# A planner's order searched anew, a shorter wait for the first weight combinations, and unit 1's layernorm statistics on another engine

## The chip, the cores and the metric

The kernel runs on one core of a Trainium2 chip. A core has a matrix engine (TensorE, PE in the profile; its weight loads are shown as PEld), a vector engine (VectorE, DVE), a scalar engine (ScalarE, ACT), a general engine (GpSimd, POOL) and a sync engine (SyncE, SP), which here does little but issue transfers. Each engine works through its own list of instructions in order and waits on semaphores; transfers run on 16 DMA engines. The metric is the device time of one execution in microseconds, as the median of several runs.

## The reference

Two layers, each of them a block of dilated local attention and a feed-forward block, on 2048 tokens of 1024 features. Each query looks at 8 keys, at distances 0, 2, ..., 14 behind it.

```python
def _layernorm(x, axis=-1, eps=1e-5):
    m = jnp.mean(x, axis=axis, keepdims=True)
    v = jnp.var(x, axis=axis, keepdims=True)
    return (x - m) / jnp.sqrt(v + eps)

def _A_ref(x, wqkv, wo):                      # H = 32, Dh = 32, W = 8, dil = 2
    qkv = (x @ wqkv).reshape(B, S, 3, H, Dh)  # then split into q, k, v by head
    idx = pos[:, None] - jnp.arange(W) * dil
    kg, vg = k[idx], v[idx]                   # idx < 0 is masked
    logits = jnp.einsum("bhsd,bhswd->bhsw", q, kg) * Dh ** -0.5
    o = jnp.einsum("bhsw,bhswd->bhsd", softmax(logits), vg)
    return o @ wo

def _B_ref(x, w1, b1, w2, b2):                # F = 3584
    r = relu(x @ w1 + b1)
    return (r * r) @ w2 + b2

x = A_x
x = x + _A_ref(_layernorm(x), A_wqkv, A_wo)
x = x + _B_ref(_layernorm(x), B_w1, B_b1, B_w2, B_b2)
x = x + _A_ref(_layernorm(x), A_wqkv, A_wo)
x = x + _B_ref(_layernorm(x), B_w1, B_b1, B_w2, B_b2)
```

## The kernel before

**Units.** The tokens are split into even and odd ones, so that the dilation becomes a window of 8 neighbours, and then into blocks of 512. A layer has four blocks, so there are eight units, 0 to 7; a unit has four tiles of 128 tokens. A unit passes through: `SA` (load x, layernorm, transpose into `xnA`), `SQ` or `SQ7` (the products for q, k and v), `S2` (attention), `SW` or `SW7` (the output projection with wo, the residual, the second layernorm, transpose into `xnB`), `SF1` (first feed-forward product, relu, square) and `SF2` (second one, and the output). The attention of unit u+1 is woven into the feed-forward block of unit u: attention is VectorE's work, the products are PE's.

**Seven products.** Most matrix products are done as 2 x 2 blocks with seven block products instead of eight. For that, sums and differences of weight blocks are needed. They are made once, from the weights as they are first loaded, by VectorE into tiles `tv` (lines L531 for wqkv, L680 for w1, L457 for w2, L1108 for wo), stored to scratch tensors in DRAM (`sk`, `sqv`, `sw`, `tw`, `two`), and loaded again by later units. The sums and differences of the other operand are the tiles `T` (L699) and `TA` (L703). For the k weights this is done in unit 0 by `keep_wqkv`: eight combinations of 128 x 1024, each followed by a store of 256 KB.

**The opening.** Unit 0's tiles are taken in the order 0, 1, 3, 2. Tiles 0, 1 and 3 get their statistics on VectorE (BATCH_NORM_STATS2 at L791, aggregate at L793) and are normalised there (L788); tile 2 goes over ScalarE. All four are transposed on PE (L807) and copied to `xnA` (L812, named `ptc` in the plan).

**Layernorm, two ways.** `ln` has a flag `vec`. With it, VectorE makes the statistics (two of L732 and one of L741 for each tile), ScalarE the inverse root (L736, L737), VectorE the normalisation (L740). Without it, ScalarE makes the statistics in two passes over the tile with a sum beside each (L746, L750, each with a read of the accumulator; L747 between them) and the inverse root (L753, L754); VectorE normalises (L759). In `SW` and `SW7` the flag is `u in STAT`. The transposes of later units are DMA transposes issued by SP (L772).

**Logits.** `S2` multiplies q with the shifted k in 16-bit products `P` (L950, 128 x 2048), eight of them for each half block, adds them up in a tree of depth `DEP0[hb]` for unit 0 (L958), and sums what is left over the features on PE with a matrix of ones (L965, four matmuls for each remaining tile). With depth 2, two tiles are left of eight; with depth 3, one.

**The order.** Nothing is issued as the functions run. Each operation is recorded in a `Plan` with an engine, a duration, what it reads and writes and a priority. `emit` first disturbs the priorities with a list of seeds (`shift`), lets `schedule` place the operations on the engines by a simple model with a limited number of buffers, and then, for each further list in `ORDER`, takes the start times of that placement as priorities, disturbs them again (`reshift`) and places anew. The last placement is the order of the instructions in every engine's list, SP's transfers included, and it also decides which buffer each tile gets. So the seeds in `ORDER` decide all orders, and nothing else in them does anything. A search outside the kernel found them.

Lines that the prediction speaks of: L663 are the matmuls of all seven-product steps, L888 those of the plain q, k, v products, L1084 those of the output projection, L485 and L1388 those of the second feed-forward product, L1057 the copies out of PSUM (`yxa`, `yxo`, `yxm`) that feed the residual additions, L1496 the difference of the two halves of the bias b2 (`b2d`), L422 every plain transfer. `xt` are the x tiles loaded for the first layernorm of a unit.

Of the kernel before, what the change touches and what calls it, by code (L numbers as in the profile page):

```python
# [26 lines left out]
ONPE = (0,)  # L27
FOLD = (0, 1, 2)
DEN = (0,)
STAT = (1, 2, 3, 4, 5, 6, 7)  # L30
NORM = (3,4,5,6,7)
EQ = True
QW = 1
# [12 lines left out]
KEEP = {"k": 0, "q": 1, "v": 1}  # L46
WO7 = (2, 3, 4, 5, 6)
KWO = 1
DEP0 = (2, 2)
NEARLY = 4  # L50
PLAIN1 = 1
HALF = 8
# [6 lines left out]
AGF = True  # L59
FNO = True  # L60
CPA = (1,)
TAIL = True
CPT = ("xn3",)
PR1 = 20.0
# [3 lines left out]
GZ = 6  # L68

ORDER = [  # L70
# [6 lines left out]

MM = 0.2157
MMH = 0.1091
# [10 lines left out]
def act(n):  # L90
    return 0.05 + n * 0.00084
# [242 lines left out]
class _Kernel:  # L334
# [465 lines left out]
    def transpose(self, xn, xnT, tl, prio, parts=1, act=False):  # L800
# [3 lines left out]
        for i in range(parts):  # L804
# [3 lines left out]

            on_act = act or parts > 1 and i in CPA

# [16 lines left out]
    def SA(self, u):  # L827
        p = self.p
        layer, b = divmod(u, self.NB)
        st = self.state.setdefault(u, {})  # L830
        xnT = Buf("8K", "xnA1" if u == 1 else "xnA", [128, 4, self.KD, 128], F16)
        st["xnA"] = xnT
        after = [self.state[u - 2].get("gatef") or self.state[max(u - 2, 1)].get("gatev")] if u >= 2 else ()
        first, rst = (), []
        for tl in ORD if u == 0 else range(4):
            t = b * 4 + tl
            x, xv = self.load_x(layer, t, after, tag="x0" if u == 0 else "xt", prio=PR1 if u == 1 else -1e6 if u == 0 else None,
                                eng="ACT" if u == 0 and tl in XACT else "SP")
            if u == 0 and tl in LNA:
                self.ln(x, xv, [0], xnT, tl, LNP, False, on_pe=True, tag="xn3", after=rst, vnorm=tl in LNV)  # L840
            elif u == 0:
                bn, ag, r, rest = self.ln_first(x, xv, xnT, tl, first)
                rst.append(r)
                if tl == 0:
                    first, rest0 = [ag] if AGF else [bn], rest
                elif tl == 1:
                    rest0([ag])
                    c, xn, no = rest()
                    first = [no if FNO else c]
                    self.keep_clock(NPB, xn)  # L850
                else:
                    rest()
            else:
                self.ln(x, xv, [0], xnT, tl, PR1 if u == 1 else 20.0, False, vnorm=u in NORM)

    def SQ(self, u, jobs, order=None, halves=()):
        nc, p = self.nc, self.p
        layer, b = divmod(u, self.NB)
        KD, NCH, D = self.KD, self.NCH, self.D
        st = self.state[u]  # L860
        xnT = st["xnA"]
        offs = {"q": 0, "k": HALO, "v": HALO}
        ws = {}
        for nm in jobs:
            self.qkv_buf(u, nm)
            ws[nm] = [Buf("8K", "w", [128, 2, 2, 4, 256], BF) for _ in range(2)]
        pieces = u == 0 and len(jobs) > 1
        for ms in range(4) if pieces else (0, 2):
            for nm in jobs:
                w = ws[nm][ms // 2]  # L870
                if pieces:
                    self.dma(lambda w=w, ms=ms: w[:, ms % 2].rearrange("p a k n -> p (a k n)"), lambda nm=nm, ms=ms: self.wqkv_block(nm, ms), (),
                             [(w, ms % 2)], 0.53, name="w")
                else:
                    self.dma(lambda w=w: w[:].rearrange("p s a k n -> p s (a k n)"),
                             lambda nm=nm, ms=ms: self.wqkv_block(nm, ms, 2).rearrange("(s p) m -> p s m", p=128), (), [(w, 0), (w, 1)], 1.06, name="w")
        if order is None:
            order = [(nm, c0) for nm in jobs for c0 in range(NCH)]

        def chunk(nm, c0, hs, parts=1):  # L880
            pq = Buf("ps", "pq", [128, BLK], F32)
            w, dst, off = ws[nm][c0 // 4], st[nm], offs[nm]
            t0, t1 = hs[0], hs[-1] + 1
            n = KD // parts

            def fm(i):
                for kd in range(i * n, (i + 1) * n):
                    nc.tensor.matmul(pq[:, t0 * HB:t1 * HB], w[:, c0 // 2 % 2, kd // 4, kd % 4, c0 % 2 * 128:c0 % 2 * 128 + 128],  # L888
                                     xnT[:, 2 * t0:2 * t1, kd, :], start=(kd == 0), stop=(kd == KD - 1))
            for i in range(parts):  # L890
                xc = [(xnT, t if i == parts - 1 else (t, i)) for t in range(2 * t0, 2 * t1)]
                st["gate" + nm] = self.pe(4 * len(hs) / parts, lambda i=i: fm(i), xc + [(w, c0 // 2 % 2)], [(pq, h) for h in hs], name="pq")
            p.add("ACT", act(HB * len(hs)), lambda: nc.scalar.copy(dst[:, c0, off + t0 * HB:off + t1 * HB], pq[:, t0 * HB:t1 * HB]),
                  [(pq, h) for h in hs], [(dst, (c0, h)) for h in hs], 2.0, name="cast")

        for nm, c0 in halves:
            chunk(nm, c0, (0,), 2 if (nm, c0) == halves[0] else 1)
        for nm, c0 in order:
            chunk(nm, c0, (0, 1))
            yield  # L900
        for nm, c0 in halves:
            chunk(nm, c0, (1,))
        for nm in jobs:
            if u == KEEP[nm]:
                self.keep_wqkv(nm, ws[nm], [op for op in self.p.ops if op.name == "ptc"] if u == 0 else ())
            self.halo_out(u, nm)

    def qkv_buf(self, u, nm):
# [152 lines left out]
    def SW(self, u):  # L1061
# [12 lines left out]
        for tl in range(4):  # L1074
# [18 lines left out]
            st["xm"].append(xm)  # L1093
            self.ln(xm, lambda xm=xm: xm[:], [0, 1], xnT, tl, 1.0, u in STAT, on_pe=u in ONPE)
        if u == KWO:
# [21 lines left out]
    def SW7(self, u):  # L1117
# [25 lines left out]
        def cells(k2, m2):  # L1143
            return [(o, (k2 * h + c, m2)) for c in range(h)]
# [6 lines left out]
        def mul(left, lc, w, right, bank, start):  # L1151
            for q in range(2):
                def fm(q=q):
                    for j in range(h):
                        nc.tensor.matmul(bank[q][:], left(j, q), right(j), start=start and j == 0, stop=j == h - 1, skip_group_check=True)  # L1155
                self.pe(h, fm, lc + [(w, 0)], [(bank[q], 0)], name="py")

        def block(k2, m2):
            return lambda j, q: o[:, k2 * h + j, m2 * HB + q * 128:m2 * HB + (q + 1) * 128]

        def T(i):
            return ts[i // 2], lambda j: ts[i // 2][:, i % 2, j, :]
# [31 lines left out]
        for q in range(2):  # L1194
            self.ln(xm[q], lambda q=q: xm[q][:], [0, 1], xnT, q, 1.0, u in STAT, on_pe=u in ONPE)
        mul(block(0, 1), cells(0, 1), *T(2), X, False)
# [5 lines left out]
        for q in range(2):  # L1202
            self.ln(xm[q + 2], lambda q=q: xm[q + 2][:], [0, 1], xnT, q + 2, 1.0, u in STAT, on_pe=u in ONPE)

# [154 lines left out]
    def SF2(self, u):  # L1359
# [21 lines left out]
        def mul(name, left, lcells, banks, start, split=False):  # L1381
            for half in range(2):
                w = self.w2_rhs(name, half)
                for q in range(2):
                    def fm(lo=0, hi=BLK, w=w, q=q, half=half):
                        for j in range(g):
                            jj = half * g + j
                            nc.tensor.matmul(banks[q][:, lo:hi], left(jj, q), w[:, j, lo:hi], start=(start and jj == 0), stop=(jj == h - 1),  # L1388
                                             skip_group_check=True)
                    if split and half and q and TAIL:  # L1390
                        xr = xm[3]
# [58 lines left out]
    def out_tile(self, layer, t, db, py, xm, end=False):  # L1450
# [5 lines left out]
        o = lambda: xm[:].bitcast(BF)  # L1456
        if end and TAIL:
            for i in range(2):
# [54 lines left out]
    def build(self):  # L1513
# [9 lines left out]
        self.biases()  # L1523
        self.S2(0, DEP0)
        for u in range(NU):
# [88 lines left out]
```

## Time and profile before

| | |
|---|---|
| median of 3 runs | 1137.02 us (1135.94 to 1138.26) |
| the profiled execution | 1142.31 us |
| its span, first to last instruction | 1140.6 us |
| PE, DVE, ACT busy | 1121.8, 995.5, 814.0 us |
| moved by DMA | 362.35 MB, mean 318 GB/s |
| granted TensorE clock, mean | 0.999 |

The profile is of one execution. Its page gives busy time by engine, then the span in 40 equal slices of 28.5 us with a digit for the busy tenths of each, then queues, the chain of work that ended last, and the costliest groups of instructions. A group's line shows the source line, the engine, what is written and read, the shapes, the count, then busy time and mean duration, then the time for which the engine idled just before such instructions and what ended that. A line of waits reads: engine, tile and line that waited, what it waited for, total us, times, longest. A matmul's own mean (379 ns for 128 x 512) is longer than its share of busy time, since matmuls overlap.

### The profile page before, as it was taken

To read this page: it belongs to the slowest core of one execution; us is meant where nothing else is said; L and a number is where in the kernel's file an instruction comes from. 1 tells how busy PE (TensorE), PEld (TensorE's weight loads), DVE (VectorE), ACT (ScalarE), POOL (GpSimd) and SP (SyncE) were. 2 spreads that over 40 slices of the span, in tenths; PEclk is the share of its full clock that TensorE was granted. 3 is DMA by queue.
4 is the path that set the end of the run, shared out by engine and by line. 5 is a ranking of instruction groups with operands and counts; after the bars stand their busy time and mean duration, and the time that the engine had idled before them with its cause. 6 is when DMAs were issued, how large, how long until landed. Compare 5 with 4: busy or idle time off the path is not lost.

```text
span 1140.6 us, 20659 instructions
## 1 busy us (share of the span) xinstructions
PE 1121.8 (98%) x7857; PEld 771.2 (68%) x7904; DVE 995.5 (87%) x1528; ACT 814.0 (71%) x1628; POOL 1.8 (0%) x8
## 2 busy tenths in 40 slices
PE   8999999998999999999999999999999999999998
PEld 6645864676846787468864688557884678845864
DVE  7999999998997899979999699995999989996341
ACT  7747896566984689757994669847698478943961
POOL 0000000000000000000000000000000000000000
PEclk9999999999999999999999999999999999999999
DMA  9965699999999996999879997899979999589981
GB/s 356 285 217 220 225 317 291 346 343 342 364 339 386 345 377 228 333 396 328 357 281 322 412 335 303 309 310 393 359 271 325 372 354 413 209 304 313 367 299 62
DMA packets 137022, 362.35 MB, mean 318 GB/s; under 512 B 67418, under 2 KB 68570, under 8 KB 116570
## 3 DMA queue, kind: packets, MB, share of 16 engines
q1 hardware_dynamic: 136778, 360.95, 91.3%
q8 instruction: 62, 1.02, 0.4%
q14 instruction: 38, 0.31, 0.1%
q10 hardware_dynamic: 144, 0.07, 0.0%
HBM read 314.84 MB, written 31.46 MB: 304 GB/s over the span
## 4 chain that ended last, share of the span: by engine, by line
PE 64%; ACT 12%; DMA 7%; DVE 2%; issue 1%; SPq 0%; ACTq 0%; DVEq 0%
PE X L663 20%; PE X L1388 12%; PE Z L663 10%; PE Z L1388 6%; PE Y L663 5%; PE X L1155 3%; ACT r L1323 3%; PE Y L1388 3%; ACT rr L1329 2%; PE py L1084 2%; PE Z L1155 1%; DMA w<-in_A_wo_dram 1%; DMA w<-sw 1%; DMA xt<-xs 1%; ACT u L1292 1%
## 5 line engine op out<-in xcount | busy, mean ns | idle before, releaser
L663 PEld LDWEIGHTS <-w 128*128 128x128 f16 (+1 forms) x4904 | 480.4, 98 | 75.9 <-DMA w<-sw 3.0
L1388 PEld LDWEIGHTS <-r 128*128 128x128 f16 x1183 | 115.6, 98 | 136.4 <-issue 3.7
L1388 PE MATMUL X<-w,r 128*128 128x512 f16 (+2 forms) x784 | 177.9, 377 | 1.4 <-ACT yxa L1057 1.0
L950 DVE TENSOR_TENSOR P<-q,k 128x2048 f16<-128x2048 f16 x128 | 154.5, 1225 | 2.2 <-ACT q L626 2.0
L663 PE MATMUL X<-T,w 128*128 128x256 f16 x1224 | 154.0, 273 | 0.1
L1029 DVE TENSOR_TENSOR pr<-pb,v 128x4096 f16<-128x4096 f16 x64 | 146.3, 2297 | 0.4 <-PE Z L663 0.2
L958 DVE TENSOR_TENSOR P<-P,P 128x2048 f16<-128x2048 f16 x110 | 134.2, 1220 | 0.1
L1323 ACT ACTIVATE r<-rr 128x1024 f16<-128x1024 f16 x110 | 123.9, 1139 | 0.3
L1036 DVE TENSOR_TENSOR pr<-pr 128x2048 f16<-128x2048 f16 (+1 forms) x128 | 118.0, 954 | 0.0
L663 PE MATMUL X<-TA,w 128*128 128x256 f16 x864 | 107.6, 273 | 0.0
L596 ACT COPY Y<-X 128x512 f32<-128x512 f32 x115 | 70.2, 610 | 26.0 <-PE X L663 21.5
L888 PE MATMUL pq<-xnA,w 128*128 128x256 f16 (+1 forms) x512 | 86.1, 326 | 2.3 <-DMA w<-in_A_wqkv_dram 0.9
L1302 ACT CAST y<-Z 128x512 f16<-128x512 f32 x110 | 69.5, 646 | 10.5 <-PE Z L663 10.1
L888 PEld LDWEIGHTS <-w 128*128 128x128 bf16 x512 | 49.8, 98 | 34.7 <-issue 1.8
L1306 DVE TENSOR_TENSOR rr<-u,y 128x512 f16<-128x512 f16 x110 | 46.1, 423 | 27.7 <-ACT y L1302 12.8
L663 PE MATMUL X<-xnB,w 128*128 128x256 f16 x440 | 56.9, 277 | 0.0
L1329 ACT ACTIVATE rr<-Y,b1T 128x256 f16<-128x256 f32 x110 | 54.4, 537 | 3.1 <-PE Y L663 2.3
L663 PE MATMUL Y<-xnB,w 128*128 128x256 f16 x440 | 56.4, 273 | 0.0
L663 PE MATMUL Z<-T,w 128*128 128x256 f16 x392 | 51.0, 274 | 4.6 <-DMA w<-sw 2.7
L614 ACT CAST u<-X 128x512 f16<-128x512 f32 x72 | 41.7, 586 | 19.3 <-PE X L663 18.5
L1329 ACT ACTIVATE rr<-X,b1T 128x256 f16<-128x256 f32 x110 | 54.6, 560 | 0.3 <-PE X L663 0.3
L618 ACT CAST yq<-Z 128x512 f16<-128x512 f32 x72 | 41.9, 585 | 16.3 <-PE Z L663 16.3
(168 smaller groups left out, 1653.4 us busy)
## 6 DMA issues: line engine op xcount, KB each, us to landing
w<-sw SPq DMA_DIRECT2D x49, 1024.0 KB, 10.2
w<-tw SPq DMA_DIRECT2D x56, 896.0 KB, 6.6
w<-in_B_w_dram SPq DMA_DIRECT2D x42, 896.0 KB, 6.2
w<-in_B_w_dram SPq DMA_DIRECT2D x35, 1024.0 KB, 10.1
w<-in_A_wqkv_dram SPq DMA_DIRECT2D x32, 1024.0 KB, 10.3
w<-sqv SPq DMA_DIRECT2D x24, 1024.0 KB, 10.9
w<-in_B_w_dram SPq DMA_DIRECT2D x28, 512.0 KB, 5.7
w<-sk SPq DMA_DIRECT2D x12, 1024.0 KB, 7.7
```

The lines of the kernel that those rows point to most:

```text
L596: self.p.add("ACT", act(512), lambda: self.nc.scalar.copy(Y[:], X[:]), [(X, 0)], [(Y, 0)], UP, name="u")
L663: nc.tensor.matmul(bank[:, a, :], lw[:, k, a * 128:(a + 1) * 128], rhs(k), start=(start and k == 0 and a == 0), stop=(k == 3), skip_group_ ...
L888: nc.tensor.matmul(pq[:, t0 * HB:t1 * HB], w[:, c0 // 2 % 2, kd // 4, kd % 4, c0 % 2 * 128:c0 % 2 * 128 + 128], xnT[:, 2 * t0:2 * t1, kd, ...
L950: nc.vector.tensor_tensor(cur[:], q[:, c, None, hb * HB:(hb + 1) * HB].to_broadcast([128, W, HB]), _win_ap(k[:, c, :], HALO + hb * HB, HB) ...
L958: nc.vector.tensor_tensor(other[:], other[:], cur[:], ALU.add)
L1029: p.add("DVE", dve(4096), lambda pr=pr, ch=ch: nc.vector.tensor_tensor(pr[:], pb[:].unsqueeze(1).to_broadcast([128, 2, W, HB]), _win_ap2(v ...
L1036: nc.vector.tensor_tensor(dst, pr[:, :, 0:n, :], pr[:, :, n:2 * n, :], ALU.add)
L1302: p.add("ACT", act(512), lambda: nc.scalar.copy(y[:], bank[:]), [(bank, 0)], [(y, 0)], 1.5, name="y")
L1306: p.add("DVE", dve(512), lambda: nc.vector.tensor_tensor(r[:, :, m, :], us[i][:], y[:], ALU.add), [(us[i], 0), (us[i], 1), (y, 0)], [(r, ( ...
L1323: p.add("ACT", 0.955, lambda: nc.scalar.activation(out=r2[:, f:f + 2, :].rearrange("p a t -> p (a t)"), in_=r[:].rearrange("p a m t -> p ( ...
L1329: p.add("ACT", 0.36, lambda a=a: nc.scalar.activation(out=r[:, a, 0, :], in_=bank[:, a, :], func=ACTF.Relu, bias=self.b1T[:, f + a:f + a + ...
L1388: nc.tensor.matmul(banks[q][:, lo:hi], left(jj, q), w[:, j, lo:hi], start=(start and jj == 0), stop=(jj == h - 1), skip_group_check=True)
```

## The change

In the words that come with it: "Order searched anew with every transfer also modelled as landing late; first k combinations wait only for the second tile; unit 1's statistics on VectorE". In the code it is this:

```diff
-STAT = (1, 2, 3, 4, 5, 6, 7)
+STAT = (2, 3, 4, 5, 6, 7)
...
-DEP0 = (2, 2)
+DEP0 = (2, 3)
...
+AFTK = True
...
 ORDER = [
-    [254407839, 254101347, ..., 254651009, ],
-    [254887702, 254542295, ..., 254633564]]
+    [291170133, 291483325, ..., 291274799, ], [291072305, 291809209, ..., 291708481, ],
+    [291835106, 291584461, ..., 291674658, ], [291087832, 291905654, 291120734, 291208902]]
...
                     c, xn, no = rest()
                     first = [no if FNO else c]
+                    self.opened = [no]
                     self.keep_clock(NPB, xn)
...
             if u == KEEP[nm]:
-                self.keep_wqkv(nm, ws[nm], [op for op in self.p.ops if op.name == "ptc"] if u == 0 else ())
+                self.keep_wqkv(nm, ws[nm], () if u else self.opened if AFTK else [op for op in self.p.ops if op.name == "ptc"])
```

- `ORDER` has other seeds: four lists (59, 23, 25 and 4 seeds) in place of two (52 and 23). The order of the instructions on every engine, and the use of buffers, is another one from the opening on. What the search modelled does not stand in the kernel; `schedule` and its constants are the same.
- The k combinations of unit 0 depend on the normalisation of tile 1 (`no`), no longer on the copies of all four transposed tiles.
- Unit 1 is no longer in `STAT`, so in its output projection `vec` is false: the statistics of its second layernorm are made on ScalarE. Before, they were made on VectorE.
- The second half block of unit 0's logits is added up to one tile in place of two: one addition more on VectorE, four matmuls fewer on PE.

All else, the products, transfers and their sizes, is the same.

15 rows, old and new, of the table ORDER are left out of this document.

## The prediction

> **What bounds the kernel now.** I read the page's first part, then busy time by stretches, then the waits of TensorE, then the chain of waits.
>
> ```profile
> span 1140.6 us, 20659 instructions
> PE 1121.8 (98%) x7857; PEld 771.2 (68%) x7904; DVE 995.5 (87%) x1528; ACT 814.0 (71%) x1628; POOL 1.8 (0%) x8
> ```
>
> TensorE (PE) idles for 1140.6 - 1121.8 = 18.8 us in all. That is all an order of instructions can win, beside the few matmuls taken out. Where it idles, and at what clock:
>
> ```profile
> 0.00:15.00 15.00, 11.31 (x78) 6.75 (x79) 8.03 (x23) 8.43 (x21) 1.75 (x8) 1.00 0.87 313
> 15.00:28.50 13.50, 13.50 (x129) 12.05 (x127) 12.17 (x14) 11.85 (x29) 0.00 (x0) 1.00 1.03 404
> 28.50:205.00 176.50, 175.23 (x1072) 104.03 (x1078) 172.98 (x224) 126.94 (x266) 0.00 (x0) 1.00 0.85 263
> 205.00:215.00 10.00, 10.00 (x68) 6.38 (x66) 10.00 (x20) 7.05 (x13) 0.00 (x0) 1.00 0.83 269
> 215.00:250.00 35.00, 33.47 (x244) 23.84 (x244) 35.00 (x53) 21.91 (x45) 0.00 (x0) 1.00 1.07 355
> 250.00:277.00 27.00, 25.09 (x227) 21.87 (x225) 24.07 (x40) 18.90 (x38) 0.00 (x0) 1.00 1.07 327
> 277.00:280.00 3.00, 0.26 (x4) 0.01 (x1) 3.00 (x6) 1.73 (x4) 0.00 (x0) 1.00 1.02 403
> 280.00:285.00 5.00, 5.00 (x31) 3.84 (x32) 3.02 (x4) 2.38 (x5) 0.00 (x0) 0.66 1.01 415
> 285.15:313.67 28.52, 28.47 (x252) 24.57 (x251) 26.89 (x38) 28.49 (x62) 0.00 (x0) 1.00 0.92 364
> 427.73:456.24 28.51, 28.46 (x230) 22.44 (x230) 26.02 (x39) 28.48 (x61) 0.00 (x0) 1.00 0.65 228
> 1112.09:1140.60 28.51, 24.35 (x119) 11.53 (x118) 4.16 (x10) 5.45 (x10) 0.00 (x0) 1.00 0.17 61
> ...
> PE Z L663 <- DMA w<-sw: 2.7, 1, 2.7
> PE Z L663 <- DVE T L699: 1.9, 1, 1.9
> PE py L1084 <- DMA w<-in_A_wo_dram: 1.4, 1, 1.4
> PE X L1388 <- ACT yxa L1057: 1.0, 1, 1.0
> PE pq L888 <- ACT q L893: 0.9, 1, 0.9
> PE Z L1388 <- ACT yxa L1057: 0.3, 1, 0.3
> ```
>
> In the stretches the numbers are length, then busy PE, weight loads, VectorE (DVE), ScalarE (ACT), POOL, then granted clock, DMA share, GB/s. Start (15.00 - 11.31 = 3.7) and tail (28.51 - 24.35 = 4.2) are waits that every order has. What is left is the six waits, 2.7 + 1.9 + 1.4 + 1.0 + 0.9 + 0.3 = 8.2 us, and the stretch behind the longest, where the clock was 0.66: 5.00 x 0.34 = 1.7 us. Three of the waits and the low clock lie between 215 and 285, in unit 1's output projection and first feed-forward product. There the DMA share is at least 1.01 in every row from 215 to 285, so the transfers are the limit, and they land one after another:
>
> ```profile
> 216.29 8.19 DMA w<-in_A_wo_dram
> 251.74 10.78 DMA xnB<-xn
> 264.88 15.06 DMA w<-sw
> 279.99 1.41 PE Z L663 x8
> 735.92 6.87 DMA xt<-xs
> ...
> ACT xn L746 <- DMA xt<-xs: 16.2, 4, 6.0
> ```
>
> The chain of waits (start, length, what) says it in order: the second wo load is issued at 216.29, and the sw load issued at 264.88 took 15.06 us to land, behind the transfers issued before it; PE went on at 279.99. Until about 215 VectorE, not DMA, is full (10.00 of 10.00), and it is VectorE that frees the buffer for the second wo load.
>
> **The point that decides.** In the order of the changed program that same sw load is again first used with 6,088 matmuls still to come, just as many as before. If its landing still holds PE, whatever is won or lost ahead of it is wiped out, and the end moves with the landing. So I cost each part first by what it does to that landing.
>
> **First k combinations (L531).** Before, they waited until all four tiles of unit 0 were transposed; now until the second is normalised. The opening:
>
> ```profile
> 9.56 0.20 DVE L793 BATCH_NORM_AGGREGATE sm<-st 128x2 f32<-128x12 f32 x1
> 10.36 0.55 DVE L788 TENSOR_SCALAR xn<-x,sm 128x1024 f16<-128x1024 bf16 x1 [0.60 <-ACT sm L785]
> 12.54 1.05 PE L888 MATMUL pq<-xnA,w 128*128 128x256 f16 x8 [0.94 <-DMA w<-in_A_wqkv_dram]
> 13.42 0.61 PE L807 MATMUL pt<-ident,xn 128*128 128x128 f16 x8
> 14.07 0.69 DVE L812 COPY xnA<-pt 128x1024 f16<-128x1024 f16 x1 [3.16 <-PE pt L807]
> 19.35 1.29 DVE L531 TENSOR_TENSOR tv<-w 128x1024 f16<-128x1024 bf16 x2
> 25.41 0.69 DVE L1496 TENSOR_TENSOR b2d<-b2b 128x512 f32<-128x512 bf16 x1 [1.29 <-DMA b2b<-in_B_b_dram]
> ```
>
> In the changed order three of them stand on VectorE between the third tile's aggregate (done 9.76) and its normalisation, the fourth behind it. They need the third 512 KB piece of weights; the fourth piece released PE at 12.54, and 0.52 MB at 404 GB/s is 1.3 us, so the third landed near 11.2 (estimate). VectorE waits there from 9.76, works 1.29 + 0.69 until 13.2, normalises until 13.7 and does the fourth by 14.4. Queued behind this wait is the normalisation; PE waits for it. But PE's order has one more group of eight matmuls (1.05) ahead of these transposes: it gets there at about 14.3, not 13.42. So PE is not held, by 0.6 us; without that cover, 13.7 - 13.42 = 0.3. The tile's copy moves from 14.07 to about 15.0: 0.9 later with four combinations done (about 2.6 us), so VectorE is 1.7 us ahead; and b2d, now nine instructions further on, should lose its 1.29 us wait. Together 3.0. The four stores now stand on SP ahead of and among the next weight loads, holding the first of these for some 2 us; its first matmul is behind 200 others, so this costs nothing.
>
> **DEP0 and the statistics.**
>
> ```profile
> L965 PE MATMUL lg<-P,grp 128*128 128x512 f16 x72 | 19.8, 379 | 0.0
> L958 DVE TENSOR_TENSOR P<-P,P 128x2048 f16<-128x2048 f16 x110 | 134.2, 1220 | 0.1
> L732 DVE BATCH_NORM_STATS2 bs<-xm 128x6 f32<-128x512 f16 x56 | 37.8, 689 | 0.5
> L741 DVE BATCH_NORM_AGGREGATE sm<-bs 128x2 f32<-128x12 f32 x28 | 5.5, 204 | 0.2
> L746 ACT ACTIVATE xn<-xm 128x1024 f16<-128x1024 f16 x4 | 4.2, 1051 | 0.0
> L750 ACT ACTIVATE xn<-xm,sm 128x1024 f16<-128x1024 f16 x4 | 4.6, 1149 | 0.0
> L750 ACT ACTIVATION_READ_ACCUMULATOR xn<-xm,sm 128x1 f32 x4 | 0.8, 190 | 0.0
> L747 ACT ACTIVATE sm<-sm 128x1 f32<-128x1 f32 x33 | 6.7, 203 | 1.1
> ```
>
> Four matmuls go (4 x 19.8/72 = 1.1 us of PE), one tree addition comes (1.22 us of VectorE), both in unit 0. PE's 1.1 us lies ahead of the deciding point: 0 in the sum; it would be -1.1 were that wait gone. VectorE's lead shrinks to 3.0 - 1.2 = 1.8.
>
> Taking 1 out of STAT moves unit 1's statistics to **ScalarE**, though the change's words say VectorE: eight BATCH_NORM_STATS2 and four aggregates leave VectorE (8 x 0.689 + 4 x 0.204 = 6.3 us), and ScalarE gets 4 x (1.05 + 0.19 + 1.15 + 0.19 + 0.20) = 11.1 us; the small Ln/Exp pairs and the normalisation stay. ScalarE has 35.00 - 21.91 = 13 us free in 215 to 250 and 8 after it; a PSUM copy may sit up to 1.3 us behind one of these, which the wait at the sw load hides (without it, up to 4 x 1.3). The four transposes of unit 1 can go out earlier, but they add no bytes. 0 in the sum.
>
> **The new order.** VectorE is busy 172.98 of 176.50 us from 28.5 to 205 and all of 205 to 250, so its 1.8 us reach the combinations that free the second wo buffer: that load goes out up to 1.8 earlier (bounds -1.8 and 0). Against it, 35 transfers ran from the one behind it to the sw load; now 36, with one more 256 KB store: 0.26 MB at 327 GB/s = +0.8 (bounds 0 and 0.8). Landing: -1.8 + 0.8 = **-1.0**.
>
> What the low clock does depends on how the waits fall. The 1.9 us wait was followed by clock 1.00, the 2.7 us wait by 0.66. In the changed order PE needs the second wo load 16 matmuls sooner, so more is waited there and perhaps less at the sw load: between -1.7 (no low clock) and +1.7 (a second one). I take 0, since waits on both sides of these two lengths are likely. The Trainium skill (TensorE: Matmul & The Clock Gate, Part 1) puts the loss at one idle window of about 3.4 us, free-running; here 2.7 us were enough, which such a window does not forbid. By 3.4 us as a plain threshold this term would be 0 to -1.7.
>
> Late in the kernel ScalarE waited four times for xt loads issued no sooner than it came to them; two of these made the 1.0 and 0.3 us waits on yxa. In the changed order two to seven groups of matmuls (about 1.5 us each) lie between the release of those buffers and ScalarE's turn, where none to two did; earlier loads, in the passes of units 1 and 2, come closer (13 groups to three, six to three). Bounds -1.3 and +1.0; I take **-1.0**.
>
> Sum: -1.0 + 0 - 1.0 = **-2.0 us**, a span of 1138.6. The profiled execution took 1142.31 in all against a median of 1137.02; the difference applied to the median gives **1135.0**. By all bounds: -1.8 - 1.7 - 1.3 = -4.8 to +0.8 + 1.7 + 1.0 = +3.5, so 1132.2 to 1140.5.
>
> **Rivals.**
> *The transfer-bound stretch dissolves.* Stores issued earlier and transposes out sooner let the sw load land before PE needs it. Then the waits of 2.7, 1.9, 1.4 and 0.9 and the low clock go, with the four matmuls: up to 9.7; with two thirds of it, -6.5: **1130.5**. For it: the DMA share was only 0.83 in 205 to 215. Against it: the same bytes must still pass, at a share above 1 for 65 us.
> *ScalarE becomes the bound at the crossing into the second feed-forward product.* In the stretches at 285 and 428, and at that place in each unit, ScalarE is busy 28.49 and 28.48 of 28.5. A new order that sets one more pair of evacuations (about 0.85) ahead of the squares PE waits for holds PE each time, from where ScalarE has no idle time left: 6 x 0.85 = 5.1 behind the deciding point, so -2.0 + 5.1 = +3.1: **1140.1**. For it: no slack in those rows. Against: none of the six crossings shows in PE's waits before.
> *The change does not do what it says:* the statistics go the other way, and spacing transfers for lateness does nothing where they are bandwidth-bound: within 0.5 us, **1137**.
>
> **How the numbers follow.** The measurement of this kernel can tell about 0.2% (2.3 us) from no change, so faster is under 1134.7 and slower over 1139.3. Forecast case 0.42 (its value lies near the edge: 0.22 faster, 0.20 same); dissolving 0.20, all faster; ScalarE 0.30 (0.28 slower, 0.02 same); nothing 0.08 (0.06 same, 0.02 slower). Faster 0.42, same 0.28, slower 0.30. The forecast's own range is 1132.2 to 1140.5; with the first rival's 1130.5 and a little beyond the second, 1130 to 1141.5.
>
> **What would show it.** Right: a sw load again holds PE near 279, with DMA share about 1 from 215; the second wo load issued near 214.5; VectorE's idle before 28.5 at most 5.5 us instead of 15.00 - 8.03 + 13.50 - 12.17 = 8.3; L732 x48; the yxa waits under 0.5. Wrong: no wait on sw, or PE waits on ACT at L1388 summing to over 3 us, or PE held at the third tile's transposes near 14.

## The result, and the profile after

The changed kernel takes 1133.39 us (median of 7 runs, 1131.52 to 1136.32) against 1137.09 us (7 runs, 1135.64 to 1138.86) of the kernel before: a ratio of 0.9969, 95% interval 0.9954 to 0.9984, or 3.7 us less. A second series gave 0.9971 (0.9960 to 0.9982; 1133.77 against 1137.10).

The two profiled executions differ by more, and mislead: the one of before, 1142.31 us, is slower than every run of these series, the one of after, 1131.52 us, is the fastest of its seven. Both kernels were therefore profiled a second time (e1 and e5 below), and what follows rests on both profiles of each.

The page of after, its first part:

```profile
span 1129.8 us, 20632 instructions
PE 1118.8 (99%) x7854; PEld 770.4 (68%) x7900; DVE 990.3 (88%) x1517; ACT 824.1 (73%) x1648; POOL 1.8 (0%) x8
```

Busy time by stretches of after (length, then PE, weight loads, VectorE, ScalarE, POOL, then granted clock, DMA share, GB/s):

```profile
0.00:15.00 15.00, 12.34 (x81) 7.24 (x82) 9.87 (x26) 7.55 (x19) 1.76 (x8) 1.00 0.85 320
15.00:28.50 13.50, 13.50 (x130) 12.15 (x128) 13.47 (x14) 12.98 (x32) 0.00 (x0) 1.00 1.03 404
...
205.00:215.00 10.00, 10.00 (x76) 7.32 (x75) 10.00 (x17) 6.79 (x13) 0.00 (x0) 1.00 1.04 315
215.00:250.00 35.00, 33.43 (x243) 23.83 (x245) 32.19 (x45) 28.63 (x60) 0.00 (x0) 1.00 1.05 363
250.00:277.00 27.00, 27.00 (x246) 23.82 (x244) 26.93 (x41) 23.50 (x50) 0.00 (x0) 1.00 1.06 373
277.00:280.00 3.00, 3.00 (x30) 2.69 (x29) 3.00 (x6) 3.00 (x7) 0.00 (x0) 1.00 1.01 423
```

The waits of PE in after, without three of the opening and one of 0.3 us on TA, with the lines shifted by four or five (L663 is L667, L1084 is L1089, L1388 is L1393, L732 is L736):

```profile
PE py L1089 <- DMA w<-in_A_wo_dram: 1.4, 1, 1.4
...
PE Y L1393 <- ACT Y L600: 0.2, 1, 0.2
PE pt L811 <- DVE xn L792: 0.2, 1, 0.2
PE X L1393 <- ACT X L502: 0.2, 1, 0.2
```

PE idles 1129.8 - 1118.8 = 11.0 us, where it idled 18.8. The wait on the third sw load (2.7), the one on T (1.9), the low clock behind them, the one on q (0.9) and those on yxa (1.0 and 0.3) are gone, though the DMA share is still above 1 from 205 to 285; the wait on the second wo load has stayed. PE is busy all of 250 to 280.

### The profile page after: what moved, and what is told of

Read it like the earlier page. It is cut to its first block, busy times and chain, and to the rows that moved or that the text cites. A ratio compares the mean times of both kernels' runs of the same rounds, so it can differ in the third digit from the quotient of the medians.

```text
span 1129.8 us, 20632 instructions
## 1 busy us (share of the span) xinstructions
PE 1118.8 (99%) x7854; PEld 770.4 (68%) x7900; DVE 990.3 (88%) x1517; ACT 824.1 (73%) x1648; POOL 1.8 (0%) x8
## 3 DMA queue, kind: packets, MB, share of 16 engines
q8 instruction: 62, 1.02, 0.4%
## 4 chain that ended last, share of the span: by engine, by line
PE 72%; DVE 15%; ACT 7%; DMA 3%; issue 2%; SPq 0%; DVEq 0%
PE X L667 19%; PE X L1393 12%; PE Z L667 10%; PE pq L893 6%; PE Z L1393 6%; PE Y L667 5%; PE py L1089 4%; DVE P L955 3%; PE Y L1393 3%; PE X L1160 3%; DVE P L963 3%; ACT r L1328 2%; DVE pr L1034 2%; PE Z L1160 1%; ACT rr L1334 1%
## 5 line engine op out<-in xcount | busy, mean ns | idle before, releaser
L667 PEld LDWEIGHTS <-w 128*128 128x128 f16 (+1 forms) x4904 | 479.8, 98 | 69.6 <-issue 0.5
L1393 PEld LDWEIGHTS <-r 128*128 128x128 f16 x1183 | 115.8, 98 | 135.4 <-issue 1.1
L1393 PE MATMUL X<-w,r 128*128 128x512 f16 (+2 forms) x782 | 176.3, 377 | 0.6 <-ACT X L502 0.2
L667 PE MATMUL X<-T,w 128*128 128x256 f16 x1224 | 151.7, 273 | 0.0
L1328 ACT ACTIVATE r<-rr 128x1024 f16<-128x1024 f16 x110 | 123.8, 1137 | 0.3
L1041 DVE TENSOR_TENSOR pr<-pr 128x1024 f16<-128x1024 f16 (+1 forms) x128 | 118.0, 956 | 0.1
L667 PE MATMUL X<-TA,w 128*128 128x256 f16 x864 | 108.4, 273 | 0.0
L600 ACT COPY Y<-X 128x512 f32<-128x512 f32 x115 | 71.2, 619 | 18.8 <-PE X L667 14.9
L667 PE MATMUL Y<-xnB,w 128*128 128x256 f16 x440 | 56.4, 273 | 0.0
L1062 ACT CAST yxo<-X 128x512 f16<-128x512 f32 x27 | 15.4, 587 | 56.0 <-PE X L1393 56.0
L618 ACT CAST u<-X 128x512 f16<-128x512 f32 x72 | 41.8, 587 | 18.8 <-PE X L667 17.4
L667 PE MATMUL X<-xnB,w 128*128 128x256 f16 x440 | 55.5, 273 | 0.0
```

What stands on the lines that cost most here:

```text
L600: self.p.add("ACT", act(512), lambda: self.nc.scalar.copy(Y[:], X[:]), [(X, 0)], [(Y, 0)], UP, name="u")
L667: nc.tensor.matmul(bank[:, a, :], lw[:, k, a * 128:(a + 1) * 128], rhs(k), start=(start and k == 0 and a == 0), stop=(k == 3), skip_group_ ...
L1041: nc.vector.tensor_tensor(dst, pr[:, :, 0:n, :], pr[:, :, n:2 * n, :], ALU.add)
L1328: p.add("ACT", 0.955, lambda: nc.scalar.activation(out=r2[:, f:f + 2, :].rearrange("p a t -> p (a t)"), in_=r[:].rearrange("p a m t -> p ( ...
```

## The experiments

The kernels below were made in two ways. In one (e8, e9, e10) the order of all operations is exactly that of before or after, and only what some operations do is edited. In the other (e2, e3, e4, e6, e7) a part of the change is put in or taken out, and the **order is carried over**: `ORDER` and its seeds give way to a list `PRIO` with the start of each operation in the placement of the base, an operation that the base lacks gets the time at which its inputs are done, and the placement is made once. For an unedited base this gives its own order back. With a part edited, about 80 of some 4,660 operations change their place among those of their engine in e3, and 190 to 280 in the others; such a run therefore measures the part together with how well the order suits it. Lines in kernels with `PRIO` are 13 to 17 lower.

### e1: the kernel before, again

No edit.

> The kernel before, unchanged, for a second profiled execution: which of the waits that were gone in the changed kernel's profile belong to the program, and which to the one execution that was profiled (1142.31 us, 5.2 over the median of the rounds). If they belong to the program: PE waits again for a sw load near 279 for 2 us or more, on T (L699) for 1 to 2 us near 267, and on the second wo load for about 1.4; second wo load issued at 216.3, within 0.5; span 1139 to 1141. If they belong to the execution: the sw wait is under 1 us, no stretch with a clock under 0.95, span about 1137.1 - 1.7 = 1135.4, and the six waits sum to 3 to 5 us in place of 8.2.

Measured: ratio 0.9994 (0.9985 to 1.0002), profiled at 1135.84 us. PE's longest waits, without those of the opening, and the stretch that had the low clock:

```profile
PE Z L663 <- DMA w<-sw: 2.1, 1, 2.1
...
PE Z L663 <- DVE T L699: 1.1, 1, 1.1
PE py L1084 <- DMA w<-in_A_wo_dram: 0.9, 1, 0.9
PE X L1388 <- ACT yxa L1057: 0.9, 1, 0.9
```

```profile
280.00:285.00 5.00, 5.00 (x48) 4.49 (x47) 5.00 (x8) 5.00 (x11) 0.00 (x0) 1.00 1.01 423
```

The places are the program's, the sizes the execution's: sw, T, wo and yxa again, 5.0 us in all in place of 7.3, no wait on q, and no low clock. Neither expectation came whole: the waits stayed, but the second wo load went out at 214.6, not 216.3, and the span is 1134.1. So the low clock (1.7 us) and some of the idle time in the first profile belong to that execution and not to the order.

### e5: the changed kernel, again

No edit.

> The changed kernel, unchanged, for a second profiled execution. If the waits on T and on the third sw load are gone by the order: again none over 0.7 us between 240 and 290, second wo load issued near 211.7, third sw load landed near 271.6, ratio 0.996 to 0.998. If the profiled execution was a lucky one (1131.52 was the lowest of its seven): a wait of 1 to 3 us on T, on a sw load or on wo, span 1131.7 (1133.39 - 1.7) or more.

Measured: ratio 0.9971 (0.9960 to 0.9982), profiled at 1136.19 us, 2.4 over its median. Its only wait over 0.6 us outside the opening, the chain's row of the second wo load (issue, length) there, and the stretch behind that wait:

```profile
PE py L1089 <- DMA w<-in_A_wo_dram: 4.2, 1, 4.2
```

```profile
214.96 8.39 DMA w<-in_A_wo_dram
```

```profile
223.30:229.00 5.70, 5.60 (x18) 2.63 (x18) 4.61 (x8) 1.66 (x3) 0.00 (x0) 0.52 1.02 420
```

Half the expectation each: no wait on T or sw here either; but the second wo load went out at 214.96, 3.3 us later than in the first profile (211.68), PE waited 4.2 us for it, and worked at a clock of 0.52 for the 5.7 us behind (5.70 x 0.48 = 2.7 us lost). What the order took from the later waits can come back at this one.

How much room the new order leaves shows where PE starts on the third sw load, here in the first profile of after:

```profile
272.99 1.04 PE L667 MATMUL Z<-T,w 128*128 128x256 f16 x8
```

The load had landed at 271.6, 1.3 us ahead of PE. In e5 it landed at 273.8, 4.4 us ahead of PE, which started there only at 278.25, 5.3 us later than in the first profile. A PE that came at 273.0 would have waited some 0.8 us for it (an estimate). So the wait on sw is gone, but by about 1 us, and in e5 also because PE was held further up.

Where the table below comes from, for the first profile of after: the chain's row of the second wo load (issued at 211.68, landed 9.04 later); SP's row of the third sw load in the timeline; and, in the view of DMA issues over that moment, its time to landing, 12.3 us.

```profile
211.68 9.04 DMA w<-in_A_wo_dram
```

```profile
259.35 0.38 SPq L426 DMA_DIRECT2D w<-sw  x1
```

```profile
w<-sw SPq DMA_DIRECT2D x1, 1024.0 KB, 12.3
```

In the same way for the others, in us from the start of the span:

| | second wo load issued | landed | third sw load landed | between the landings |
|---|---|---|---|---|
| before, first profile | 216.3 | 224.5 | 279.9 | 55.5 |
| before, e1 | 214.6 | 222.5 | 276.5 | 54.0 |
| before's order, thin statistics (e8) | 215.3 | 223.6 | 277.8 | 54.2 |
| before's order, plain copies (e10) | 215.4 | 223.6 | 270.8 | 47.2 |
| after, first profile | 211.7 | 220.7 | 271.6 | 50.9 |
| after, e5 | 215.0 | 223.4 | 273.8 | 50.4 |
| after's order, stores twice (e9) | 213.4 | 222.3 | 282.2 | 60.0 |
| old parts, searched (e11) | 213.8 | 222.5 | 274.6 | 52.1 |

### e2 and e7: the parts without the order, the order without the parts

e2 carries the order of before over to the three parts:

```diff
-STAT = (1, 2, 3, 4, 5, 6, 7)
+STAT = (2, 3, 4, 5, 6, 7)
-DEP0 = (2, 2)
+DEP0 = (2, 3)
+AFTK = True
-ORDER = [...]
+PRIO = [...]      # starts in before's placement
```

> The three parts (k combinations early, unit 1's statistics on ScalarE, one more tree addition) in the order of before: every operation has as priority its start in before's placement, and the placement is made once. Theory order (the parts gain only because the search placed everything anew for them): not faster than before, 1137 to 1141, with new waits of 3 us or more on PE, not at the places of before's. Theory parts (VectorE's lead and its relief do it by themselves): faster than before by 2 us or more, no wait on T or sw over 0.5 us.

Measured: 1141.90 us against 1136.70, ratio 1.0052 (1.0037 to 1.0067). Its longest waits:

```profile
PE X L650 <- DMA w<-in_B_w_dram: 1.9, 1, 1.9
PE py L472 <- DMA sw<-tv: 1.3, 1, 1.3
```

e7 is the other way round: `STAT`, `DEP0` and the early k combinations as before, `PRIO` from after's placement.

> All three parts undone, the changed kernel's order carried over. Theory order by itself (the search has found a better placing, parts or not): 1133 to 1135.5, ratio 0.996 to 0.9985. Theory fit (parts and order only gain together): as slow as before or slower, ratio 0.9995 to 1.006, with the lost time in waits of PE that the kernel before does not have. Theory parts add up (e3 gave back 2.1 us, e4 1.7, the four matmuls 1.1): 1.1 + 2.1 + 1.7 = 4.9 over the changed kernel, ratio 1.001.

Measured: 1140.01 us, ratio 1.0025 (1.0011 to 1.0039). One wait stands out:

```profile
PE Z L649 <- DVE T L685: 5.4, 1, 5.4
```

So neither the parts in before's order nor the changed order without its parts gains: 0.5% slower with the parts alone (some 5 us by the medians), 0.25% with the order alone (2.9), 0.3% faster together. e7 lies within the range of theory fit. In e2 theory order has the direction right, but the time lies above its 1137 to 1141, and no wait reached its 3 us. In e2 the waits are many, small and mostly at places that before does not have; in e7 the one on T is back, larger than ever. Both are orders carried over, with over 200 operations moved, so neither says what a search for its parts would have found (e11 below does so for the old ones).

### e3, e4, e6: one part taken back out of the changed kernel

Each carries after's order over. e3 puts unit 1's statistics back on VectorE (`STAT` with 1), e4 makes the k combinations wait for all four tiles (`AFTK = False`), e6 sets `DEP0 = (2, 2)`.

> The changed kernel with its order carried over, unit 1's statistics back on VectorE. Theory statistics (6.3 us off VectorE between 215 and 260 bring T, the normalisations and the transposes forward, and so the sw load): VectorE is busy all of 215 to 250 again (35.0 in place of 32.2), PE waits on T or on a sw load between 240 and 290 for 2 to 4 us, time 1136 to 1138. Theory lead (the opening's gain in VectorE is what brings them forward): the waits stay under 0.7 us in all in that stretch, time within 1 us of the changed kernel's, 1132.5 to 1134.5.

> The changed kernel with its order carried over, the first k combinations again behind all four transposed tiles. Theory lead: VectorE idles 7 us or more before 28.5 (4.6 before the edit... 28.5 - 9.87 - 13.47 = 5.2 in the changed kernel), the second wo load goes out 2 us or more later than 211.68, PE waits on T or on a sw load between 240 and 290 for 2 us or more, time 1135.5 to 1138. Theory statistics: the second wo load later, but no such wait over 0.7 us, and 1132.5 to 1134.5.

> The changed kernel with its order carried over, the second half block of unit 0 again added up to two tiles: four matmuls more on PE, one addition fewer on VectorE. Theory of the sum (only the matmuls count, now that no sw wait follows them): +1.1 us over the changed kernel, 1134 to 1135. Theory fit (whatever is taken out, the order no longer fits and gives back 2 us, as with the other two parts): ratio to before 0.998 to 0.9995, so 2 us or more over the changed kernel, with a new wait of 1 us or more on PE. If the addition weighed on VectorE: its load earlier, second wo load issued before 211, and no slower than the changed kernel.

Measured: e3 0.9988 (0.9977 to 0.9999), e4 0.9984 (0.9973 to 0.9995), e6 0.9973 (0.9960 to 0.9987). The longest waits of each between 40 and 290, e3 first:

```profile
PE py L1072 <- DMA w<-in_A_wo_dram: 2.5, 1, 2.5
...
PE Z L650 <- DVE T L686: 0.6, 1, 0.6
```

```profile
PE lg L953 <- DVE P L946: 1.6, 1, 1.6
```

```profile
PE Z L650 <- DVE T L686: 2.1, 1, 2.1
PE py L1072 <- DMA w<-in_A_wo_dram: 1.9, 1, 1.9
```

Taking out the statistics or the early combinations gives back 1.9 and 1.5 us by the ratios against 0.9971, with intervals that overlap the changed kernel's; taking out the tree addition gives back 0.2, which its interval (some 1.5 us either way) cannot tell from nothing nor from the 1.1 us of its theory of the sum. None of the three showed its theory's places. e3's T wait was 0.6, not 2 to 4; e4's VectorE idled 7.4 us before 28.5 as foreseen (28.5 - 7.67 - 13.43) and its second wo load went out at 215.1, but the sw wait was 0.9, and its longest was one on VectorE at 57 us (L953). Where e4's loss sits is not shown: the profiled execution took 1133.06 us, 2.7 under e4's median and no more than the changed kernel's. e6's, at 1136.06, is 2.2 over its median, so its two waits may be larger than in most executions. That VectorE's lead or its relief is by itself what clears the later waits is not shown by these.

### e8: before's order, VectorE relieved

```diff
-    def ln(self, x, xv, xcells, xnT, tl, prio, vec, ..., parts=1):
+    def ln(self, x, xv, xcells, xnT, tl, prio, vec, ..., parts=1, few=512):
...
-                p.add("DVE", dve(512, False), lambda sg=sg: nc.vector.bn_stats(out=bs[:, sg, :], in_=xv()[:, sg * 512:(sg + 1) * 512]),
+                p.add("DVE", dve(512, False), lambda sg=sg: nc.vector.bn_stats(out=bs[:, sg, :], in_=xv()[:, sg * 512:sg * 512 + few]),
...
-            self.ln(xm, ..., u in STAT, on_pe=u in ONPE)
+            self.ln(xm, ..., u in STAT, on_pe=u in ONPE, few=16 if u == 1 else 512)
```

> The kernel before, its order exactly as it was; the eight BATCH_NORM_STATS2 of unit 1's second layernorm read 16 columns in place of 512 (so that the variance is that of a sample: part of the computation is left out). That takes some 8 x 0.5 = 4 us off VectorE between 225 and 260 and puts nothing on ScalarE. Theory relief (VectorE's time there holds back the normalisations, the transposes and so the sw load behind them on SP): the last xnB transpose goes out 2 us or more before 259.0 (255 to 257 in this kernel's other execution, less 2), the third sw load lands by 274.5, waits on T and sw sum to under 2 us in place of 3.2 to 4.6, ratio 0.9965 to 0.9985. Rival (the landing is set by the bytes ahead of the load alone): third sw load landed 62 to 64 us after the second wo load's issue, waits on T and sw over 2.5, ratio 0.999 to 1.001.

Measured: 1136.78 us, ratio 1.0001 (0.9987 to 1.0014). The stretch in which VectorE was full, and the waits:

```profile
215.00:250.00 35.00, 33.55 (x245) 23.90 (x245) 32.19 (x56) 21.92 (x45) 0.00 (x0) 1.00 1.08 356
```

```profile
PE Z L663 <- DMA w<-sw: 2.0, 1, 2.0
PE Z L663 <- DVE T L699: 1.4, 1, 1.4
PE py L1084 <- DMA w<-in_A_wo_dram: 1.3, 1, 1.3
```

VectorE is busy 32.19 of 35.00 us, just as in after, and the rest is as before: the same three waits, 54.2 us between the landings. From the wo load's issue to the sw load's landing it was 277.8 - 215.3 = 62.5 us, within the rival's 62 to 64. Theory relief is refuted for before's order. The wait that is booked to VectorE (T L699) is not VectorE's load either: in 250 to 277 of before's first profile VectorE was busy 24.07 of 27.00 us, and in both profiles of before it waited for the transposed tile itself, with the same row:

```profile
DVE T L699 <- DMA xnB<-xn: 1.3, 1, 1.3
```

### e9: after's order, more to transfer

```diff
+        self.two2 = [tc.dram_tile([128, 2, 4, BLK], F16, name=f"twp{i}") for i in range(2)]
...
                 self.dma(lambda: self.two[i // 2][:, i % 2, c0:c0 + 2, :], lambda: t[i][:], ...)
+                op, one = p.ops[-1], p.ops[-1].fn
+
+                def twice():
+                    one()
+                    nc.sync.dma_start(self.two2[i // 2][:, i % 2, c0:c0 + 2, :], t[i][:])
+                op.fn = twice
```

> The changed kernel, its order exactly as it was; each of the eight 256 KB stores of wo combinations is issued twice, the second time to a scratch that nobody reads. Seven of them stand ahead of the third sw load: 7 x 0.26 MB at 363 GB/s = 5.0 us more of transfers. Theory transfers (the stretch from 215 to 285 is full of them, and their landing decides when PE gets on): the third sw load lands 3 to 5 us later, PE waits for T or a sw load 2 to 5 us in that stretch, ratio 0.999 to 1.0015. Rival (transfers there have slack in the new order): it lands later, but the waits in 240 to 290 stay under 1 us, ratio 0.9965 to 0.9982.

Measured: 1141.06 us, ratio 1.0035 (1.0022 to 1.0047), 7.3 us over the changed kernel (1133.77). Waits, then the stretch behind the wait on wo, and the one in and behind the wait on T:

```profile
PE X L668 <- DVE T L704: 3.1, 1, 3.1
PE py L1090 <- DMA w<-in_A_wo_dram: 2.6, 1, 2.6
PE X L668 <- DMA w<-in_B_w_dram: 1.7, 1, 1.7
PE Z L668 <- DMA w<-sw: 1.6, 2, 0.9
```

```profile
222.20:227.50 5.30, 5.19 (x21) 2.50 (x21) 4.87 (x6) 1.66 (x3) 0.00 (x0) 0.68 1.02 420
...
266.50:270.00 3.50, 0.38 (x4) 0.19 (x3) 1.23 (x5) 0.88 (x3) 0.00 (x0) 1.00 1.08 267
270.00:273.00 3.00, 3.00 (x26) 2.37 (x26) 3.00 (x4) 1.64 (x4) 0.00 (x0) 1.00 0.97 396
```

Theory transfers holds, and the price is above its range (1.0015) and above the bytes: 9 to 10 us more between the landings for 5.0 us of bytes, T 3.1, the w1 load 1.7 and sw 1.6 us. The new order has little slack for transfers either; the prediction's picture of a stretch that transfers limit is right for both kernels.

### e10: before's order, plain copies for the transposes

```diff
         def f5():
-            nc.sync.dma_start_transpose(xnT[:, tl], xn[:])
+            if plain:
+                nc.sync.dma_start(xnT[:, tl], xn[:].rearrange("p (k t) -> p k t", t=128))
+            else:
+                nc.sync.dma_start_transpose(xnT[:, tl], xn[:])
...
-            self.ln(xm, ..., u in STAT, on_pe=u in ONPE)
+            self.ln(xm, ..., u in STAT, on_pe=u in ONPE, plain=u == 1)
```

> The kernel before, its order exactly as it was; the four DMA transposes into unit 1's xnB are plain transfers of the same 256 KB (so xnB holds xn untransposed and what follows is computed from that). Theory transposes (they hold the transfer engines far longer than their bytes: in the profile of before GB/s falls to 270, 297 and 168 in the three 4 us from 240 to 252 and to 275 and 277 in the two from 260, against about 415 elsewhere, 7.6 us of transfer time): the third sw load lands 47 to 50 us after the second wo load's landing in place of 54.0 to 55.5, PE waits under 0.5 us for it and for T, ratio 0.9955 to 0.998. Rival (bytes set the pace): landing within 1.5 us of 54, waits as before, ratio 0.999 to 1.001.

Measured: 1133.96 us against 1136.43, ratio 0.9976 (0.9967 to 0.9986). Two of the 4 us stretches in which the transposes stood, first in before, then in e10, and e10's longest wait on a transfer behind the opening:

```profile
240.00:244.00 4.00, 3.95 (x25) 2.31 (x24) 4.00 (x6) 2.28 (x6) 0.00 (x0) 1.00 1.22 270
...
248.00:252.00 4.00, 4.00 (x35) 3.21 (x34) 4.00 (x7) 2.40 (x6) 0.00 (x0) 1.00 1.24 168
```

```profile
240.00:244.00 4.00, 4.00 (x24) 2.06 (x22) 4.00 (x7) 2.44 (x6) 0.00 (x0) 1.00 1.04 408
...
248.00:252.00 4.00, 4.00 (x39) 3.57 (x38) 4.00 (x9) 2.99 (x7) 0.00 (x0) 1.00 1.01 393
```

```profile
PE X L1391 <- DMA w<-tw: 1.0, 1, 1.0
```

Same order, same bytes, VectorE's work untouched: the dips in GB/s are gone, 47.2 us between the landings in place of 54.2 (e8), no wait on T or sw, 2.5 us faster. So in before's order both those waits depend on the four transposes. A transpose also holds SP's queue, for 1.3 to 6.6 us each in before's first profile (6.56 at 251.74), where the plain copies of e10 hold it for 0.5 to 1.2 us. But the transfer engines did not stand idle behind that queue: from landing to landing their share was 1.07 and 1.06 in before's two profiles, against 1.02 in e10. So it is mainly the engines' time that the four transposes take up.

### e11 and e12: a search of one's own

The edit is `PRIO` alone, found outside the kernel by the search that the expectations describe.

> The three parts as before; the order searched again from before's placement (random moves of start times, about 38,000 tried, kept where the end comes earlier with transfers at a lower rate or landing 0.8 to 2 us late). Theory search (the gain is the order's, whatever the parts): ratio 0.9955 to 0.9985, second landing of wo to third sw load under 52 us. Theory parts (without them no order gets there): 0.999 or more, waits on T, sw and wo of 3 us or more in all.

> The three parts as in the changed kernel; the order searched on from its placement in the same way, some 35,000 moves. Theory search: better than the changed kernel by 1 to 3 us, ratio 0.9945 to 0.9962, waits between 215 and 285 under 1.5 us in all. If the changed order was as good as such a search gets, or the moves gain only by its own model: ratio 0.996 to 0.999.

Measured: e11 1134.13 us, ratio 0.9978 (0.9965 to 0.9990); e12 1132.86 us, ratio 0.9965 (0.9952 to 0.9978). The waits of e11 that matter, then e12's longest:

```profile
PE X L1374 <- ACT yxa L1043: 2.2, 3, 1.1
...
PE Z L649 <- DVE T L685: 0.5, 1, 0.5
```

```profile
PE py L1072 <- DMA w<-in_A_wo_dram: 3.3, 1, 3.3
```

With none of the three parts, an order searched for late landings loses the waits on sw and nearly all of the one on T: 2.5 us of the change's 3.7. (Its landings are 52.1 us apart, just over the 52 expected.) Searching on from the changed order gained nothing that can be told from the changed kernel, and its wait on wo stayed, in an execution 2.8 us over its median. What the parts are worth beyond the search, 3.7 - 2.5 = 1.2 us between kernels whose intervals overlap, is not settled. No kernel here beats the changed one beyond doubt.

## Why the prediction was right, and where it was not

Faster was the forecast, by 2.0 us at 1135.0; it came to 3.7 at 1133.4, inside the likeliest case's own range (1132.2 to 1140.5). But its deciding point did not hold: "no wait on sw", the first of its own signs of being wrong, came. That the time lies near the forecast is in part luck. At its end the stretch dissolved, as in the first rival: the waits on sw and T are gone. At its start it tightened: in e5 a longer wait on wo and the low clock behind it took that gain back, and the sum had both at nothing.

**The step that failed** is the second term of the landing: "Against it, 35 transfers ran from the one behind it to the sw load; now 36, with one more 256 KB store: 0.26 MB at 327 GB/s = +0.8 (bounds 0 and 0.8)". It counts transfers by bytes at one rate. Measured from landing to landing, the same stretch shrank from 55.5 and 54.0 us to 50.9 and 50.4, about -4 us, though one transfer more was issued in it. The stretches, before's two profiles first, then after's two:

```profile
224.50:279.90 55.40, 50.76 (x399) 38.97 (x399) 52.47 (x84) 36.87 (x73) 0.00 (x0) 1.00 1.07 341
222.50:276.50 54.00, 50.76 (x399) 38.90 (x399) 51.00 (x81) 37.01 (x73) 0.00 (x0) 1.00 1.06 353
220.70:271.60 50.90, 50.74 (x402) 39.45 (x404) 48.06 (x69) 43.31 (x92) 0.00 (x0) 1.00 1.07 366
223.40:273.80 50.40, 50.29 (x374) 37.60 (x376) 45.59 (x65) 40.19 (x85) 0.00 (x0) 0.95 1.07 368
```

Length times GB/s is 18.9 and 19.1 MB in before and 18.6 and 18.5 in after: what moved between the landings became less by some 0.4 MB, about 1 us, and the other 3 us are the rate, 341 and 353 GB/s against 366 and 368. e10 shows what can hold the rate down: in before's order four transposes of 256 KB cost 7.0 us beyond plain transfers of the same size. In the first profile of before the GB/s dips around them (270, 297, 168, 275, 277 in 4 us stretches) are deeper in sum than in that of after (157, 279, 315), though both have four. That the difference between the two orders lies with the transposes is argued from these dips, not shown. That the order of transfers makes it, rather than the statistics, is what e8 (54.2 us with the statistics thinned) and e11 (52.1 in another order with the old parts) speak for; which neighbour of which transpose matters was not tried.

With that, "its landing still holds PE" fell: no sw wait in either profile of after, by the narrow room shown under e5.

**The first term**, -1.8 us for the second wo load, has the right size on average only: it went out at 216.3, 214.6, 215.3 and 215.4 in before's order (mean 215.4) and at 211.7, 215.0 and 213.4 (e9) in after's (mean 213.4), -2.0. One program varies by as much as the term. In after VectorE's lead runs into the stores of the combinations, its longest wait there between 28.5 and 215, in the first profile and then in e5:

```profile
DVE tv L535 <- DMA sqv<-tv: 3.0, 1, 3.0
```

```profile
DVE tv L535 <- DMA sqv<-tv: 3.6, 1, 3.6
```

**The opening** went as worked out: VectorE idles 28.5 - 9.87 - 13.47 = 5.2 us before 28.5 against 8.3, a lead of 3.1 where 3.0 was worked out; PE waited 0.2 us for the third tile, where 0 was forecast.

**DEP0 and the statistics at nothing**: nothing in the runs speaks against it for either as a single part (e6 against e5, 0.9973 and 0.9971; e8 1.0001). But e3 suggests, with overlapping intervals, that a part at nothing in the old order is not free to take out of the new one.

**The four matmuls**: costed at 0 as long as the sw wait stood behind them, "it would be -1.1 were that wait gone". It is gone, so by that working they count; e6, which puts them back, measured 0.2 us, and so does not show it.

**The late waits on yxa**, -1.0: the 0.9 (e1) and 1.3 us are gone, none in either profile of after.

**The clock**, 0 between -1.7 and +1.7: a stretch of low clock in one of two profiles on each side. "More is waited there", at wo, is right too: 1.4 and 4.2 us against 1.4 and 0.9.

The sum of it closes to 0.4 us, with the four matmuls at the worked-out 1.1. From e1 to after's first profile: T and sw -3.2, yxa -0.9, four matmuls -1.1, wo +0.5, in all -4.7; the spans give 1129.8 - 1134.1 = -4.3. From e1 to e5: -3.2 - 0.9 - 1.1 + 3.3 (wo) + 2.7 (clock) = +0.8; the spans, 1134.5 - 1134.1 = +0.4. The difference of the medians, -3.7, lies between.

**The rivals.** The dissolving stretch came in part: the waits on sw and T went, but the one on wo stayed, and the DMA share stayed above 1. Nor was the sw load issued sooner after the wo load (47.7 and 49.6 us behind it in after, 48.6 and 47.0 in before); it landed sooner once issued, 12.3 and 9.2 us against 15.1 and 14.9. ScalarE as the bound did not come: PE waited 0.4 us for it at L1393. "The change does not do what it says" was wrong in its reason: an order searched with transfers landing late does help where they are the limit (e11). That it helps because how transfers stand decides how long they take fits the rates above, but was not tried by itself.

## What to carry to other kernels

Count transfers in the time that they take up, not in bytes: look for stretches where the DMA share is 1 and GB/s falls, see which transfers stand there, and price them by replacing them with plain ones of the same size. An edit and the order searched for it are one thing; judge a part by searching anew without it, not by taking it out. When a wait is cleared, look for the one that grows ahead of it, and for how little the landing now comes before its use. And profile the same program twice before explaining a difference of half a per cent: here single waits moved by 3 us between executions.

## What the runs showed of the hardware

A DMA transpose of 128 x 1024 in 16 bits, among other transfers that fill the queue, cost about 1.75 us more than a plain transfer of its 256 KB (7.0 us for four, 54.2 in e8 to 47.2 in e10). With 0.64 us for 0.26 MB at 408 GB/s that is an estimate of some 2.4 us in all, so about 0.11 TB/s. The Trainium skill (Advanced Engine Details and Errata, X-Bar Transpose (TRN2)) has transposes as fast as regular DMAs; these two runs do not agree with that.

The clock fell after waits of 2.7 (before), 2.6 (e9), 3.3 (e12), 4.2 (e5) and 5.4 us (e7), and not after 3.1 (e9: 0.38 of 3.50 us busy, then 1.00) or 2.5 us (e3). So the length of the wait alone does not decide. Each time it fell to 0.50, for 3.4 us (before, e9, e12) or for twice that, 6.8 (e5, e7); in before from 280.53 to 283.94, in e5 from 221.91 to 228.73. The Trainium skill (TensorE: Matmul & The Clock Gate, Part 1) has a free-running window, which fits that a longer wait can go without loss; its length there, about 3.4 us, is that of the low clock here, but more than the 2.6 us of waiting that were enough; so the prediction's remark that such a window does not forbid a fall after 2.7 us holds only if the window need not be idle throughout.
